# Attention with hashed buckets and two MLPs on one core: loads, bits, placing, conversions and the last copies in another order

## The chip, the cores and the metric

One core of a Trainium2 chip runs the whole program in one launch. Its engines are TensorE (PE, with its weight loads as PEld), VectorE (DVE), ScalarE (ACT), GpSimd (POOL) and SyncE (SP, which here only issues DMA transfers, in the order of the program). Each engine works through its own list of instructions in order and waits on semaphores for the others. The metric is the device time of one execution, in microseconds (us).

## The reference

Three stages: attention and two MLPs. The weights of the MLPs are float64 and reach the kernel as 64-bit words; all other inputs are float32.

```python
def _attn_ref(q, k, v, proj):                 # q, k, v: (2, 8, 768, 64), proj: (64, 6)
    scale = 1.0 / np.sqrt(D)
    q_bits = (np.einsum('bhsd,dk->bhsk', q, proj) > 0).astype(np.int64)
    k_bits = (np.einsum('bhsd,dk->bhsk', k, proj) > 0).astype(np.int64)
    powers = 2 ** np.arange(n_bits)
    q_bucket = np.sum(q_bits * powers, axis=-1)
    k_bucket = np.sum(k_bits * powers, axis=-1)
    mask = q_bucket[:, :, :, None] == k_bucket[:, :, None, :]
    scores = scale * np.matmul(q, k.transpose(0, 1, 3, 2))
    scores = np.where(mask, scores, -1000000000.0)
    scores = scores - np.max(scores, axis=-1, keepdims=True)
    attn = np.exp(scores)
    attn = attn / (np.sum(attn, axis=-1, keepdims=True) + 1e-09)
    return np.matmul(attn, v).astype(np.float32)

def reference(...):
    attn_out = _attn_ref(**attn_kwargs)
    x = np.ascontiguousarray(attn_out.transpose(0, 2, 1, 3)).reshape(B * S, H * D)   # 1536 x 512
    h = np.maximum(x @ w_in, 0.0);  x = h * h @ w_out          # 512 -> 2048 -> 512
    h = x @ w2_in;  return (h * np.tanh(softplus(h))) @ w2_out # 512 -> 2048 -> 512
```

## The kernel before

**Pairs and steps.** The 16 heads (2 batches of 8) go in 8 pairs `p`. A pair has 12 steps (`PER`), each a tile of 128 query rows of one head against all 768 keys; there are 96 steps (`N`), in groups of three (`QT`) that share one accumulator. The loop at the end of the listing runs over the steps `j`. Every large number is kept as a rounded part and a remainder (`qh`/`ql`, `kh`/`kl`, `ph`/`pl`), and products are summed over both. One step does, in this order of the code:

- the DMA issues and GpSimd work that a table `calls` has for this step (`at(j, f)` adds to it);
- PE: `scores(j + 2)`, four matmuls from `QA`, `KA` and `QB`, `KB` (L365, L367); the last 12 rows of `QB` and `KB` hold the hash bits, so that a bucket that differs makes the score a huge number;
- ACT: `exponent(j + 1)` (L382);
- if bits are under way: their negation on ACT (L291);
- if a group of three is finished: `unstack` copies its sums out of PSUM on ACT, for the first head of a pair into `hi` (L434), for the second into `both` (L439). Only one `both` buffer exists; in the next step `place` moves its halves by DMA into `hi` and `lo` (L442, L443), and `finish` later adds and scales on GpSimd into `xf`, the input of the MLPs;
- DVE: `lower(j - 1)`, the remainder `pl` (L409), which frees the PSUM buffer of the transposes `pT`;
- if bits are under way: `compare` on DVE (L294) and one GpSimd operation (L295);
- PE: `transpose(j)`, six transposes `pT` (L392), and where a half of a pair is done the six sums as a row (L394);
- DVE: `clamp(j + 2)` (L373), which frees the PSUM buffer of the scores;
- ACT: `upper(j)`, the rounded part `ph` (L405);
- PE: `pv` of the group before (L421), four matmuls into `acc`;
- in one step of each pair: `bits_split` (L286), eight matmuls that give the next pair's hash bits, from `qh`, `ql`, `kh`, `kl`;
- the `next(conv)` calls that a list `conv_at` has for this step.

Scores, transposes and bits share three PSUM buffers (`ps2`), taken in turn.

**The next pair.** While pair `p` is worked on, pair `p + 1` is made ready by a `plan` of steps: `load` of `q_r`, `k_r` and `v_r` (L156, L161), `split_q` and `split_k` on GpSimd (L311, L312, L328 to L330: `qh`, `ql`, `kh`, `kl`) and `split_v` (L345, L346), `place_q`, `place_k` (DMA into `QA`, `KA`, `QB`, `KB`; L321, L339) and `place_bits` (L304, L305). Pair 0 has a plan of its own, since its own inputs are loaded only at the start.

**Weights.** The MLP weights arrive as 64-bit words and are turned into float32 by hand, in pieces of 128 x 512, by the generator `weights()`: a load `stg` (L83), Abs (L117 on ACT), a clamp and a shift (L121, L122 on DVE), two or-operations (L124, L126 on DVE), and two GpSimd operations that split the result (L127, L128). Each `next(conv)` advances it by one `yield`, a quarter of a piece. Five pieces are done beside the attention, the others within the MLPs.

**The end.** After the loop come the row of the last reciprocals (`rT` on PE, `rs` on ACT, L453), the last `pl`, and with `early.close()` the buffers of attention are released; `split` makes `xs` from the finished block of `xf` (L615, L616), the last sums are accumulated, and the MLPs begin with the matmuls `h` (L642 to L644).

Of the kernel before, what the change touches and what calls it, by code (L numbers as in the profile page):

```python
# [17 lines left out]
P = 128  # L18
# [9 lines left out]

LAG = 5

WARM = 3

F64_LOW = 3.4332275390625e-05
F64_HIGH = 122879.9921875
# [3 lines left out]
def lsh_attention_relu2_mish_kernel(ctx, tc, qT, kT, vP, proj, w_in, w_out, w2_in, w2_out, out):  # L38
# [16 lines left out]
    def b32(ap):  # L55
        return ap.bitcast(F32)
# [29 lines left out]
    def weights():  # L86

        pieces = [
            (i, nm, src, c)
            for i in range(2 * G)  # L90
            for nm, src in (("i", (w_in, w2_in)[i // G]), ("o", (w_out, w2_out)[i // G]))
            for c in range(FC)
        ]
        staged = {}

        def stage(k):
            if k not in staged and k < len(pieces):
                i, _, src, c = pieces[k]
                staged[k] = fetch(src, c, i % G)

        stage(0)
        yield
        for k, (i, nm, _, c) in enumerate(pieces):
            if c == 0:
                W[i, nm] = wpools[i % 2].tile([P, 2, FC, 512], F32R, tag="w" + nm, name=f"w{nm}{i}")
            t = W[i, nm]
            s = staged.pop(k)
            for n in range(k + 1, k + 1 + len(stage_pools)):
                stage(n)

            words = s.bitcast(U32).rearrange("p (n t) -> p n t", t=2)
            lo, hi = words[:, :, 0], words[:, :, 1]
            hf = s.bitcast(F32).rearrange("p (n t) -> p n t", t=2)[:, :, 1]
            m = stg.tile([P, 512], F32, tag="cv", name="cv")
            mu = m.bitcast(U32)
            if loaded[-1] == EXP_SET:
                nc.scalar.activation(m, hf, AF.Abs)  # L117
            else:
                nc.vector.scalar_tensor_tensor(m, hf, -1.0, hf, ALU.mult, ALU.max)
            yield  # L120
            nc.vector.tensor_scalar(m, m, F64_LOW, F64_HIGH, ALU.max, ALU.min)  # L121
            nc.vector.tensor_scalar(mu, mu, 3, 0x3FFFFFF8, ALU.logical_shift_left, ALU.bitwise_and)  # L122
            yield
            nc.vector.scalar_tensor_tensor(mu, lo, 29, mu, ALU.logical_shift_right, ALU.bitwise_or)  # L124
            yield
            nc.vector.scalar_tensor_tensor(mu, hi, 0xC0000000, mu, ALU.bitwise_and, ALU.bitwise_or)  # L126
            nc.gpsimd.tensor_scalar(t[:, 0, c, :], m, 1.0, 0.0, ALU.mult, ALU.add)  # L127
            nc.gpsimd.tensor_tensor(t[:, 1, c, :], m, b32(t[:, 0, c, :]), ALU.subtract)  # L128
            yield
# [16 lines left out]
    one = early.enter_context(tc.tile_pool(name="one", bufs=1))  # L146
    qk = early.enter_context(tc.tile_pool(name="qk", bufs=3))
    pm = early.enter_context(tc.tile_pool(name="pm", bufs=3))
    ps2 = early.enter_context(tc.tile_pool(name="ps2", bufs=3, space=PSUM))

    sgs, rawt, heads, vst, v_rs = {}, {}, {}, {}, {}

    def load(p, nm):

        t = raw.tile([P, S], F32, tag=nm, name=nm)
        nc.sync.dma_start(out=t, in_=(qT if nm == "q_r" else kT)[p])  # L156
        rawt[p] = rawt.get(p, ()) + (t,)
# [201 lines left out]
    def scores(j):  # L359
        p, half, hh, t = seq[j]  # L360
        QA, QBt, KA, KBt = heads[p, hh]
        q0 = half * H2 + t * P
        ps = sc[j] = ps2.tile([P, 1024], F32, tag="ps2", name="s")
        for c0, c1 in ((0, 512), (512, S)):
            nc.tensor.matmul(ps[:, c0:c1], QA[:, q0:q0 + P], KA[:, c0:c1], start=True, stop=False)  # L365
        for c0, c1 in ((0, 512), (512, S)):
            nc.tensor.matmul(ps[:, c0:c1], QBt[:, q0:q0 + P], KBt[:, c0:c1], start=False, stop=True)  # L367

# [43 lines left out]
    def pv(g, n):  # L412

        p, half, hh, _ = seq[g * QT]
        if n == 0:
            accs[g] = ps1.tile([P, H2], F32, tag="ps1", name="acc")
        per = 2 * KT // QT
        for k in range(n * per, (n + 1) * per):
            c = k % KT
            w = vst[p][:, hh * KT + c, :]  # L420
            nc.tensor.matmul(accs[g], w, phl[g][k // KT][:, c, :], start=k == 0, stop=k == 2 * KT - 1)  # L421
# [3 lines left out]
    def unstack(g, j):  # L425

        p, half, hh, _ = seq[g * QT]
        acc = accs.pop(g)
        del phl[g]
        if hh == 0:  # L430
            hi = xt.tile([P, H2], F32, tag="hi", name="hi")
            lo = xt.tile([P, H2], F32, tag="lo", name="lo")
            hl[p, half] = hi, lo
            nc.scalar.activation(hi, acc, AF.Copy)  # L434
            at(j + 1, lambda: nc.sync.dma_start(out=lo[0:D], in_=hi[D:P]))
        else:
            hi, lo = hl[p, half]
            both = xt.tile([P, H2], F32, tag="both", name="both", bufs=1)
            nc.scalar.activation(both, acc, AF.Copy)  # L439

            def place():
                nc.sync.dma_start(out=hi[D:P], in_=both[0:D])  # L442
                nc.sync.dma_start(out=lo[D:P], in_=both[D:P])  # L443

            at(j + 1, place)
            at(j + 4 + 2 * (j == N), lambda: finish(p, half))

    rbs = {}
# [28 lines left out]

    calls = {}

    def at(j, f):  # L480
        calls.setdefault(j, []).append(f)

    bits_at = {}
    for p in range(NP - 1):
        o, n = p * PER, p + 1
        if p == 0:
            plan = ((3, split_q, (n,)), (4, split_k, (n,)), (5, place_q, (n, 0)), (6, place_k, (n, 0)),
                    (6, place_q, (n, 1)), (7, place_k, (n, 1)), (8, place_bits, (n, 0)), (8, place_bits, (n, 1)),
                    (8, split_v, (n,)), (8, load, (n + 1, "q_r")), (8, load, (n + 1, "k_r")), (11, load_v, (n + 1,)))
            bits_at[o + 6] = n  # L490
        else:
            plan = ((1, place_k, (n, 0)), (2, load, (n + 1, "q_r")), (3, load, (n + 1, "k_r")), (3, split_v, (n,)),
                    (7, place_bits, (n, 0)), (7, place_q, (n, 1)), (8, place_bits, (n, 1)), (8, place_k, (n, 1)),
                    (10, load_v, (n + 1,)))
            bits_at[o + 4] = n
        plan += (9, split_q, (n + 1,)), (10, split_k, (n + 1,)), (11, place_q, (n + 1, 0))
        for m, f, args in plan:
            if args[0] < NP:
                at(o + m, lambda f=f, args=args: f(*args))

    conv_at = [5, 6, 6, 8, 10] + [b for b in bits_at if b > PER for _ in range(2)] + [N - PER + m for m in (1, 4, 6, 8)]

    kb = head_bits(0, 1, 0, S)
    head_k(0)
# [40 lines left out]
    split_v(0)  # L545
    load(1, "q_r")
    load(1, "k_r")
    load_v(1)
    split_proj()
    waiting, bits, sums = None, None, None  # L550
    for j in range(N):
        for f in calls.pop(j, ()):
            f()
        if j + 2 < N:
            scores(j + 2)
        if j + 1 < N:
            exponent(j + 1)
            sums = next((k for k, last in ends.items() if last == j + 1), None)
            if sums is not None:
                add_tiny(sums)  # L560
        if bits is not None:
            bits[0]()
        if waiting is not None:
            unstack(waiting, j)
            waiting = None
        if j:
            lower(j - 1)
        if bits is not None:
            bits[1]()
            bits = None  # L570
        if j == 1:
            head_qbits(1, 0, S, qb1)
        done = next(iter(r6s), None)
        transpose(j, r6s.get(done))
        if j + 2 < N:
            clamp(j + 2)
        if sums is not None:
            nc.vector.reciprocal(tiny[sums], tiny[sums])
            if j + 2 < N:
                r6s[sums] = tiny[sums]  # L580
            sums = None
        upper(j)
        if done is not None:
            del r6s[done]
            broadcast(*done, pts[j][:2 * QT, S:S + P], j)
        g, n = divmod(j, QT)
        if g:
            pv(g - 1, n)
            if n == QT - 1:
                waiting = g - 1  # L590
        if j == 0:
            qb1 = head_bits(1, 0, 0, S)
        if j in bits_at:
            bits = bits_split(bits_at[j])
        for _ in range(conv_at.count(j)):
            next(conv)
    for f in calls.pop(N, ()):
        f()
    ps = ps2.tile([P, 1024], F32, tag="ps2", name="rT")
    done = seq[N - 1][:2]  # L600
    r6 = tiny[done]
    nc.tensor.transpose(ps[:2 * QT, 0:P], r6, ident)
    lower(N - 1)
    broadcast(*done, ps[:2 * QT, 0:P], N)
    unstack(waiting, N)
    early.close()

    act = ctx.enter_context(tc.tile_pool(name="act", bufs=NBLK, reuse_waits="tile"))
# [7 lines left out]
            nc.vector.tensor_tensor(t[:, 1, c, :], src[:, c, :], b32(t[:, 0, c, :]), ALU.subtract)  # L616

    xs = {}
    split((0, 0), xf[0])
    for n in range(QT):  # L620
        pv(N // QT - 1, n)
    unstack(N // QT - 1, N)
    for j in sorted(calls):
        for f in calls[j]:
# [163 lines left out]
```

## Time and profile before

| | us |
|---|---|
| median of 3 runs | 762.97 (762.72 to 763.2) |
| the profiled execution | 762.05 |
| its span | 759.9 |
| PE busy | 745.8 |
| DVE busy | 534.5 |
| ACT busy | 358.0 |
| POOL busy | 263.9 |

Busy times are sums over the span of one profiled execution; 762.05 is the time of that execution itself, of which the span is the part between its first and last instruction. The mean TensorE clock granted was 0.997 of full speed.

### The profile page before, as it was taken

The page shows a single profiled execution, that of the slowest core. Times are in us where ns is not written, and L with a number is a line of the kernel's source. Part 1 is how long each engine was busy: PE and PEld are TensorE (multiplying, and loading weights), DVE is VectorE, ACT ScalarE, POOL GpSimd, SP SyncE. Part 2 cuts the span into 40 slices and gives each one's busy share as a digit, 9 for nine tenths or more (in the row PEclk, how much of TensorE's full clock was granted, in tenths as well). Part 3 has the DMA queues.
Part 4 walks back from the last instruction along what each step waited for, and adds up shares of the span by engine and source line. Part 5 has one row for each costly group of instructions (what it writes and reads, how often), then busy time and mean ns, then how long its engine had stood idle before and what let it go on. Part 6 is the DMA issues. An engine that isn't in the chain of part 4 may idle for free.

```text
span 759.9 us, 10509 instructions
## 1 busy us (share of the span) xinstructions
PE 745.8 (98%) x3742; PEld 635.5 (84%) x3742; DVE 534.5 (70%) x859; ACT 358.0 (47%) x640; POOL 263.9 (35%) x261
## 2 busy tenths in 40 slices
PE   8889999999999999999999999999999999999997
PEld 4779999999998888888888888888888888888886
DVE  8878988988997966566566688978454767566223
ACT  6878889889897443423233213333223121212120
POOL 9464555655223433232232232224223222232100
PEclk9999999999999999999999999999999999999999
DMA  5775696678423122122121122112212111120013
GB/s 145 196 207 157 167 232 158 167 203 193 108 71 92 56 84 82 57 69 70 56 84 55 56 68 67 60 56 84 84 55 81 59 56 56 56 83 28 1 55 111
DMA packets 28956, 72.69 MB, mean 96 GB/s; under 512 B 5048, under 2 KB 10264, under 8 KB 28904
## 3 DMA queue, kind: packets, MB, share of 16 engines
q1 hardware_dynamic: 28824, 72.01, 33.5%
q8 instruction: 30, 0.49, 0.3%
q14 instruction: 22, 0.18, 0.1%
q10 hardware_dynamic: 80, 0.00, 0.0%
HBM read 46.14 MB, written 3.19 MB: 65 GB/s over the span
## 4 chain that ended last, share of the span: by engine, by line
PE 86%; DMA 4%; DVE 3%; ACT 2%; POOL 2%; issue 2%; SPq 0%; DVEq 0%; ACTq 0%; POOLq 0%
PE h L642 11%; PE h L644 11%; PE h L643 11%; PE pT L392 6%; PE acc L421 6%; PE acc L688 6%; PE acc L689 6%; PE acc L690 6%; PE acc L696 6%; PE acc L695 6%; PE acc L694 6%; PE s L367 3%; PE s L365 3%; DVE pl L409 1%; ACT ph L405 1%
## 5 line engine op out<-in xcount | busy, mean ns | idle before, releaser
L643 PE MATMUL h<-xs,wi 128*128 128x512 f32 x384 | 149.4, 389 | 0.0
L644 PE MATMUL h<-xs,wi 128*128 128x512 f32 x384 | 149.4, 389 | 0.0
L642 PE MATMUL h<-xs,wi 128*128 128x512 f32 x384 | 149.4, 389 | 0.0
L668 ACT ACTIVATE g<-h 128x512 f32<-128x512 f32 x48 | 28.7, 598 | 188.7 <-PE h L644 172.0
L409 DVE TENSOR_TENSOR pl<-pT,ph 128x768 fp32r<-128x768 f32 x96 | 91.7, 956 | 20.1 <-ACT ph L405 13.4
L652 ACT ACTIVATE r<-h 128x512 f32<-128x512 f32 x48 | 28.7, 598 | 153.3 <-PE h L644 153.3
L127 POOL TENSOR_SCALAR wo<-cv 128x512 fp32r<-128x512 f32 x32 | 29.4, 918 | 194.3 <-DVE cv L126 178.9
L382 ACT ACTIVATE e<-e,nm 128x768 f32<-128x768 f32 x96 | 89.8, 936 | 6.0 <-DVE e L373 5.5
L673 DVE TENSOR_TENSOR gl<-g,gh 128x512 fp32r<-128x512 f32 x48 | 35.9, 748 | 80.6 <-ACT gh L670 80.6
L373 DVE TENSOR_SCALAR_CACHE_REDUCE e<-s 128x768 f32<-128x768 f32 x96 | 91.0, 947 | 0.9 <-PE s L367 0.8
L654 DVE TENSOR_TENSOR s<-r 128x512 f32<-128x512 f32 x48 | 38.8, 808 | 70.2 <-ACT r L652 70.2
L405 ACT ACTIVATE ph<-pT 128x768 fp32r<-128x768 f32 x96 | 77.7, 809 | 18.2 <-PE pT L394 10.1
L644 PEld LDWEIGHTS h<-xs,wi 128*128 128x128 f32 x384 | 72.1, 188 | 15.1
L642 PEld LDWEIGHTS h<-xs,wi 128*128 128x128 f32 x384 | 72.1, 188 | 14.9
L643 PEld LDWEIGHTS h<-xs,wi 128*128 128x128 f32 x384 | 72.0, 188 | 14.8
L392 PE MATMUL pT<-ident,e 128*128 128x128 f32 x576 | 79.1, 273 | 3.6 <-DVE pl L409 3.2
L127 POOL TENSOR_SCALAR wi<-cv 128x512 fp32r<-128x512 f32 x32 | 27.3, 854 | 147.5 <-DVE cv L126 147.5
L392 PEld LDWEIGHTS pT<-ident,e 128*128 128x128 f32 x576 | 66.3, 140 | 11.2 <-ACT r L386 1.9
L688 PE MATMUL acc<-gh,wo 128*128 128x512 f32 x192 | 74.7, 389 | 0.0
L689 PE MATMUL acc<-gl,wo 128*128 128x512 f32 x192 | 74.7, 389 | 0.0
L690 PE MATMUL acc<-gh,wo 128*128 128x512 f32 x192 | 74.7, 389 | 0.0
L694 PE MATMUL acc<-wo,gh 128*128 128x512 f32 x192 | 74.7, 389 | 0.0
(111 smaller groups left out, 1413.8 us busy)
## 6 DMA issues: line engine op xcount, KB each, us to landing
stg<-in_w_in_dram SPq DMA_DIRECT2D x32, 512.0 KB
stg<-in_w_out_dram SPq DMA_DIRECT2D x32, 512.0 KB
KA<-kh SPq DMA_DIRECT2D x28, 192.0 KB
v_r<-in_vP_dram SPq DMA_DIRECT2D x8, 384.0 KB
rb<-rd SPq DMA_DIRECT2D x32, 96.0 KB
out_dram<-tot SPq DMA_DIRECT2D x12, 256.0 KB
q_r<-in_qT_dram SPq DMA_DIRECT2D x7, 384.0 KB
k_r<-in_kT_dram SPq DMA_DIRECT2D x7, 384.0 KB
```

What stands on the lines that cost most here:

```text
L373: nc.vector.tensor_scalar(e, ps[:, 0:S], MASKED, None, ALU.min, ALU.min, accum_out=nm)
L382: nc.scalar.activation(e, e, AF.Exp, bias=nm, scale=-1.0, accum_out=ssums[p, half][:, c:c + 1])
L392: nc.tensor.transpose(ps[:, c * P:(c + 1) * P], e[:, c * P:(c + 1) * P], ident)
L405: nc.scalar.activation(ph, v, AF.Copy)
L409: nc.vector.tensor_tensor(pl, v, b32(ph), ALU.subtract)
L642: nc.tensor.matmul(h, w[:, 0, fi, cs], xs[:, 0, c, :], start=c == 0, stop=False)
L643: nc.tensor.matmul(h, w[:, 0, fi, cs], xs[:, 1, c, :], start=False, stop=False)
L644: nc.tensor.matmul(h, w[:, 1, fi, cs], xs[:, 0, c, :], start=False, stop=c == PPB - 1)
L688: nc.tensor.matmul(y, w[:, 0, fi, cs], gh, start=fi == 0, stop=False)
L689: nc.tensor.matmul(y, w[:, 0, fi, cs], gl, start=False, stop=False)
L690: nc.tensor.matmul(y, w[:, 1, fi, cs], gh, start=False, stop=fi == FC - 1)
L694: nc.tensor.matmul(o, gh[:, qs], w[:, 0, fi, :], start=fi == 0, stop=False)
```

## The change

- Pair 0's plan: the loads of `q_r` and `k_r` of pair 2 move from step 8 to step 4, that of `v_r` from 11 to 9; the first `place_k` of pair 1 goes from step 6 to 5, its second from 7 to 8, the bits' placing from step 8 to 7. Pair 1's bits are computed in step 5, not 6. In pair 1's plan the loads of pair 3 go from steps 2 and 3 to 4 and 5.
- The placing of `both` is put first among its step's calls.
- `next(conv)` is called between `lower(j - 1)` and the bits' comparison, not at the step's end; the first load of a weight piece goes ahead of `load_v(1)`; the steps in `conv_at` are others.
- Four of the five early weight pieces have Abs and clamp as three GpSimd operations.
- `scores(0)` has two matmuls of zeros between its two halves.
- At the end: `clamp(95)` stands ahead of `lower(92)`; the sums' copies `unstack(29)`, `unstack(30)`, the row `rs` and `unstack(31)` come among and behind the `xs` copies; the last reciprocals are made on DVE alone; the last accumulator sits in a `ps2` buffer.

```diff
+EARLY = 5
+FILL = 2
@@ weights
-            if loaded[-1] == EXP_SET:
+            if 0 < k < EARLY:
+                nc.gpsimd.tensor_scalar(m, hf, 0.0, -2.0, ALU.min, ALU.mult)
+                nc.gpsimd.tensor_tensor(m, m, hf, ALU.add)
+                nc.gpsimd.tensor_scalar(m, m, F64_LOW, F64_HIGH, ALU.max, ALU.min)
+            elif loaded[-1] == EXP_SET:
                 nc.scalar.activation(m, hf, AF.Abs)
...
-            nc.vector.tensor_scalar(m, m, F64_LOW, F64_HIGH, ALU.max, ALU.min)
+            if not 0 < k < EARLY:
+                nc.vector.tensor_scalar(m, m, F64_LOW, F64_HIGH, ALU.max, ALU.min)
@@ pools
-    ps2 = early.enter_context(tc.tile_pool(name="ps2", bufs=3, space=PSUM))
+    ps2 = late.enter_context(tc.tile_pool(name="ps2", bufs=3, space=PSUM))
@@ scores
+        for _ in range(FILL * (j == 0)):
+            nc.tensor.matmul(ps[:, 0:H2], zero[:, 0:P], zero, start=False, stop=False)
@@ unstack
-            both = xt.tile([P, H2], F32, tag="both", name="both", bufs=1)
+            if g < N // QT - 1:
+                both = xt.tile([P, H2], F32, tag="both", name="both", bufs=1)
+            else:
+                both = b32(pt.tile([P, KT, H2], F32R, tag="ph", name="both")[:, 0, :])
...
-            at(j + 1, place)
+            at(j + 1, place, j < N)
@@ calls
-    def at(j, f):
-        calls.setdefault(j, []).append(f)
+    def at(j, f, first=False):
+        c = calls.setdefault(j, [])
+        c.insert(0 if first else len(c), f)
...
         if p == 0:
-            plan = ((3, split_q, (n,)), (4, split_k, (n,)), (5, place_q, (n, 0)), (6, place_k, (n, 0)),
-                    (6, place_q, (n, 1)), (7, place_k, (n, 1)), (8, place_bits, (n, 0)), (8, place_bits, (n, 1)),
-                    (8, split_v, (n,)), (8, load, (n + 1, "q_r")), (8, load, (n + 1, "k_r")), (11, load_v, (n + 1,)))
-            bits_at[o + 6] = n
+            plan = ((3, split_q, (n,)), (4, split_k, (n,)), (4, load, (n + 1, "q_r")), (4, load, (n + 1, "k_r")),
+                    (5, place_q, (n, 0)), (5, place_k, (n, 0)), (6, place_q, (n, 1)), (7, place_bits, (n, 0)),
+                    (7, place_bits, (n, 1)), (8, place_k, (n, 1)), (8, split_v, (n,)), (9, load_v, (n + 1,)))
+            bits_at[o + 5] = n
         else:
-            plan = ((1, place_k, (n, 0)), (2, load, (n + 1, "q_r")), (3, load, (n + 1, "k_r")), (3, split_v, (n,)),
+            m = 2 if p > 1 else 4
+            plan = ((1, place_k, (n, 0)), (m, load, (n + 1, "q_r")), (m + 1, load, (n + 1, "k_r")), (3, split_v, (n,)),
...
-    conv_at = [5, 6, 6, 8, 10] + [b for b in bits_at if b > PER for _ in range(2)] + [N - PER + m for m in (1, 4, 6, 8)]
+    conv_at = [4, 6, 6]
+    for p in range(1, NP - 1):
+        conv_at += [p * PER + m for m in ((4, 6) if p % 2 else (4, 5))]
+    conv_at += [N - PER - 4, N - PER - 3] + [N - PER + m for m in (2, 3, 6)]
@@ the loop
+    next(conv)
     load_v(1)
...
-        if waiting is not None:
+        if waiting is not None and j < N - QT:
             unstack(waiting, j)
             waiting = None
+        if j == N - 3:
+            clamp(j + 2)
+        if j == N - 1:
+            done = seq[j][:2]
+            r6 = sm.tile([P, 2 * QT], F32, tag="r6", name="r6", bufs=2)
+            nc.vector.tensor_scalar(r6, ssums.pop(done), 1e-9, None, ALU.add)
+            nc.vector.reciprocal(r6, r6)
         if j:
             lower(j - 1)
+        for _ in range(conv_at.count(j)):
+            next(conv)
         if bits is not None:
             bits[1]()
...
-        for _ in range(conv_at.count(j)):
-            next(conv)
@@ the end
+    rp = ps2.tile([P, 1024], F32, tag="ps2", name="rT")[:2 * QT, 0:P]
+    nc.tensor.transpose(rp, r6, ident)
     lower(N - 1)
-    broadcast(*done, ps[:2 * QT, 0:P], N)
-    unstack(waiting, N)
+    accs[N // QT - 1] = ps2.tile([P, 1024], F32, tag="ps2", name="acc")[:, 0:H2]
+    for n in range(QT):
+        pv(N // QT - 1, n)
     early.close()
...
-    split((0, 0), xf[0])
-    for n in range(QT):
-        pv(N // QT - 1, n)
+    split((0, 0), xf[0], 0, 2)
+    unstack(waiting, N - 1)
+    for f in calls.pop(N):
+        f()
+    split((0, 0), xf[0], 2)
+    unstack(N // QT - 2, N)
+    broadcast(*done, rp, N)
     unstack(N // QT - 1, N)
```

What the edits move is seen in the order of the instructions on an engine (the lines of the changed kernel are its own, so L409 there is L420, and so on). First, SP's transfers around pair 2's loads (`q_r`, `k_r`) and pair 1's placing. Before:

```order
L156 DMA k_r<-in_kT_dram 128x768
L161 DMA v_r<-in_vP_dram 128x768
L321 DMA QA<-qh 64x768
L321 DMA QA<-ql 64x768
L321 DMA QB_126<-qh 64x768
L83 DMA stg<-in_w_in_dram 128x512
L339 DMA KA<-kh 64x768 x2
L339 DMA KB_130<-kl 64x768
L321 DMA QA<-qh 64x768
```

Of the change:

```order
L165 DMA k_r<-in_kT_dram 128x768
L87 DMA stg<-in_w_in_dram 128x512
L170 DMA v_r<-in_vP_dram 128x768
L165 DMA q_r<-in_qT_dram 128x768
L165 DMA k_r<-in_kT_dram 128x768
L87 DMA stg<-in_w_in_dram 128x512
L330 DMA QA<-qh 64x768
L330 DMA QA<-ql 64x768
L330 DMA QB_126<-qh 64x768
L348 DMA KA<-kh 64x768 x2
L348 DMA KB_130<-kl 64x768
```

Two loads of pair 2 and a second weight piece now stand ahead of the first placing; before, the loads came behind the placing of pair 1's bits. Further on, SP's transfers when the `both` of pair 0 is placed, in the first steps of pair 1. Before:

```order
L455 DMA rd<-rs 6x128
L339 DMA KA<-kh 64x768 x2
L339 DMA KB_128<-kl 64x768
L442 DMA hi<-both 64x384
L443 DMA lo<-both 64x384
L156 DMA q_r<-in_qT_dram 128x768
L156 DMA k_r<-in_kT_dram 128x768
L442 DMA hi<-both 64x384
```

Of the change:

```order
L469 DMA rd<-rs 6x128
L456 DMA hi<-both 64x384
L457 DMA lo<-both 64x384
L348 DMA KA<-kh 64x768 x2
L348 DMA KB_128<-kl 64x768
L456 DMA hi<-both 64x384
L457 DMA lo<-both 64x384
L165 DMA q_r<-in_qT_dram 128x768
```

The first two transfers of `both` go ahead of `KA` and `KB` of pair 2, and the second two ahead of the loads of pair 3. On DVE, the steps around pair 1's bits (`q_r<-bits` is the comparison, `cv` the weight piece). Before:

```order
L409 TENSOR_TENSOR pl<-pT,ph 128x6x128
L373 TENSOR_SCALAR e,nm<-s 128x768
L121 TENSOR_SCALAR cv<-cv 128x512
L122 TENSOR_SCALAR cv<-cv 128x512
L409 TENSOR_TENSOR pl<-pT,ph 128x6x128
L294 TENSOR_TENSOR q_r<-bits,k_r 48x768
L373 TENSOR_SCALAR e,nm<-s 128x768
L578 RECIPROCAL r_455<-r_455 128x6
L409 TENSOR_TENSOR pl<-pT,ph 128x6x128
L373 TENSOR_SCALAR e,nm<-s 128x768
L124 SCALAR_TENSOR_TENSOR cv<-stg,cv 128x512
```

Of the change:

```order
L384 TENSOR_SCALAR e,nm<-s 128x768
L420 TENSOR_TENSOR pl<-pT,ph 128x6x128
L130 TENSOR_SCALAR cv<-cv 128x512
L131 TENSOR_SCALAR cv<-cv 128x512
L133 SCALAR_TENSOR_TENSOR cv<-stg,cv 128x512
L303 TENSOR_TENSOR q_r<-bits,k_r 48x768
L384 TENSOR_SCALAR e,nm<-s 128x768
L420 TENSOR_TENSOR pl<-pT,ph 128x6x128
L384 TENSOR_SCALAR e,nm<-s 128x768
L607 RECIPROCAL r_465<-r_465 128x6
```

The conversion stands behind the `pl` and ahead of the comparison, with the or-operation that came three clamps later. Last, ACT at the end of attention. Before:

```order
L405 ACTIVATE ph<-pT 128x6x128 x2
L453 ACTIVATE rs<-rT 6x128
L434 ACTIVATE hi<-acc 128x384
L615 ACTIVATE xs<-xf_74 128x512 x4
L439 ACTIVATE both<-acc 128x384
L117 ACTIVATE cv<-stg 128x512
```

Of the change:

```order
L416 ACTIVATE ph<-pT 128x6x128 x2
L639 ACTIVATE xs<-xf_74 128x512 x2
L453 ACTIVATE both<-acc 128x384
L639 ACTIVATE xs<-xf_74 128x512 x2
L445 ACTIVATE hi<-acc 128x384
L467 ACTIVATE rs<-rT 6x128
L453 ACTIVATE both<-acc 128x384
L125 ACTIVATE cv<-stg 128x512
```

The `xs` copies come first, and `rs`, which was ahead of them, stands behind two copies of sums.

## Rows read from the trace of the kernel before

**Rows 1.** The page: busy us, share of the span, instructions of each engine

```profile
PE 745.8 (98%) x3742; PEld 635.5 (84%) x3742; DVE 534.5 (70%) x859; ACT 358.0 (47%) x640; POOL 263.9 (35%) x261
```

**Rows 2.** Windows: us, busy PE PEld DVE ACT POOL, clock, DMA share, GB/s

```profile
12.00:22.00 10.00, 9.48 (x54) 6.86 (x53) 9.77 (x16) 7.68 (x15) 9.42 (x15) 1.00 0.58 168
...
22.00:36.00 14.00, 12.40 (x85) 11.46 (x84) 11.45 (x20) 11.45 (x21) 5.84 (x5) 1.00 0.94 240
...
50.00:60.00 10.00, 6.79 (x34) 5.84 (x33) 5.07 (x11) 5.29 (x10) 3.81 (x3) 0.83 0.69 200
...
300.00:350.00 50.00, 50.00 (x223) 41.40 (x222) 29.29 (x48) 17.55 (x30) 15.72 (x14) 1.00 0.23 74
...
56.39:59.81 3.42, 3.42 (x14) 2.96 (x13) 2.69 (x7) 2.35 (x5) 0.00 (x0) 0.50 0.65 213
```

**Rows 3.** Timeline around pair 1's bits: start, duration, instruction, [idle before <-releaser]

```profile
22.58 1.85 POOL L330 TENSOR_TENSOR kl<-k_r,kh 128x768 fp32r<-128x768 f32 x1
...
28.66 0.67 ACT L117 ACTIVATE cv<-stg 128x512 f32<-128x512 f32 x1 [0.94 <-DMA stg<-in_w_in_dram]
...
29.37 0.43 DVE L121 TENSOR_SCALAR cv<-cv 128x512 f32<-128x512 f32 x1 [1.83 <-ACT cv L117]
...
31.27 0.84 PE L392 MATMUL pT<-ident,e 128*128 128x128 f32 x6 [1.60 <-DVE pl L409]
...
31.36 0.95 DVE L294 TENSOR_TENSOR q_r<-bits,k_r 48x768 f32<-48x768 f32 x1 [0.23 <-ACT k_r L291]
...
34.92 1.76 DVE L124 SCALAR_TENSOR_TENSOR cv<-stg,cv 128x512 uint32<-128x512 uint32 x1
...
38.57 0.84 PE L392 MATMUL pT<-ident,e 128*128 128x128 f32 x6
```

**Rows 4.** Timeline around pair 2's loads and bits

```profile
36.66 0.51 SPq L156 DMA_DIRECT2D q_r<-in_qT_dram  x1
...
40.40 1.12 POOL L311 TENSOR_SCALAR qh<-q_r 128x768 fp32r<-128x768 f32 x1 [4.27 <-DMA q_r<-in_qT_dram]
...
48.95 0.82 SPq L443 DMA_DIRECT2D lo<-both  x1
...
51.02 0.82 PE L392 MATMUL pT<-ident,e 128*128 128x128 f32 x6
...
53.42 0.49 ACT L439 ACTIVATE both<-acc 128x384 f32<-128x384 f32 x1 [3.90 <-DMA lo<-both]
...
55.75 0.58 PE L286 MATMUL bits<-qh,pwr 128*112 128x512 f32 x2 [3.21 <-POOL xf L474]
...
61.65 0.82 PE L392 MATMUL pT<-ident,e 128*128 128x128 f32 x6
```

**Rows 5.** Timeline around a later pair's bits

```profile
82.29 0.82 PE L392 MATMUL pT<-ident,e 128*128 128x128 f32 x6
...
83.78 0.65 DVE L124 SCALAR_TENSOR_TENSOR cv<-stg,cv 128x512 uint32<-128x512 uint32 x1
...
86.08 0.87 PE L392 MATMUL pT<-ident,e 128*128 128x128 f32 x6 [0.19 <-DVE pl L409]
...
88.30 0.81 PE L392 MATMUL pT<-ident,e 128*128 128x128 f32 x6
```

**Rows 6.** Timeline from the last exponent to the first matmul of the MLPs

```profile
228.64 0.94 ACT L382 ACTIVATE e<-e,nm 128x768 f32<-128x768 f32 x1 [0.24 <-DVE e L373]
...
231.44 0.27 ACT L453 ACTIVATE rs<-rT 6x128 f32<-6x128 f32 x1
...
231.98 2.18 ACT L615 ACTIVATE xs<-xf 128x512 fp32r<-128x512 f32 x4
...
233.70 0.39 PE L642 MATMUL h<-xs,wi 128*128 128x512 f32 x1
```

**Rows 7.** Timeline of the start

```profile
1.32 4.11 PE L208 MATMUL zeros<-zero 128*128 128x384 f32 x6 [1.32 <-DVE zero L184]
...
9.54 0.58 PE L367 MATMUL s<-KB,QB 128*128 128x512 f32 x2 [1.20 <-DVE QB L262]
```

More of the change, by code (lines that the diff above doesn't have):

```diff
@@ L414, in pv @@
         p, half, hh, _ = seq[g * QT]
-        if n == 0:
+        if n == 0 and g not in accs:
             accs[g] = ps1.tile([P, H2], F32, tag="ps1", name="acc")
@@ L557, in lsh_attention_relu2_mish_kernel @@
             exponent(j + 1)
-            sums = next((k for k, last in ends.items() if last == j + 1), None)
+            sums = next((k for k, last in ends.items() if last == j + 1 < N - 1), None)
             if sums is not None:
@@ L572, in lsh_attention_relu2_mish_kernel @@
             head_qbits(1, 0, S, qb1)
-        done = next(iter(r6s), None)
-        transpose(j, r6s.get(done))
-        if j + 2 < N:
+        ready = next(iter(r6s), None)
+        transpose(j, r6s.get(ready))
+        if j + 3 < N:
             clamp(j + 2)
@@ L578, in lsh_attention_relu2_mish_kernel @@
             nc.vector.reciprocal(tiny[sums], tiny[sums])
-            if j + 2 < N:
-                r6s[sums] = tiny[sums]
+            r6s[sums] = tiny[sums]
             sums = None
         upper(j)
-        if done is not None:
-            del r6s[done]
-            broadcast(*done, pts[j][:2 * QT, S:S + P], j)
+        if ready is not None:
+            del r6s[ready]
+            broadcast(*ready, pts[j][:2 * QT, S:S + P], j)
         g, n = divmod(j, QT)
@@ L588, in lsh_attention_relu2_mish_kernel @@
             pv(g - 1, n)
-            if n == QT - 1:
+            if n == QT - 1 and j < N - 1:
                 waiting = g - 1
@@ L594, in lsh_attention_relu2_mish_kernel @@
             bits = bits_split(bits_at[j])
-        for _ in range(conv_at.count(j)):
-            next(conv)
[L597 to L602, printed above, removed]
+    rp = ps2.tile([P, 1024], F32, tag="ps2", name="rT")[:2 * QT, 0:P]
+    nc.tensor.transpose(rp, r6, ident)
     lower(N - 1)
-    broadcast(*done, ps[:2 * QT, 0:P], N)
-    unstack(waiting, N)
+    accs[N // QT - 1] = ps2.tile([P, 1024], F32, tag="ps2", name="acc")[:, 0:H2]
+    for n in range(QT):
+        pv(N // QT - 1, n)
     early.close()
```

## Prediction

> **What bounds the kernel now.** I read the page's summary first: TensorE (PE) is busy 745.8 us, 98% of the span [rows 1], so only some 14 us can come from PE's idle time, and the question is where that lies. The windows say where: once the MLP part runs, PE is busy 50.00 of 50.00 us, but 12.40 of 14.00 us at 22 to 36 and 6.79 of 10.00 us at 50 to 60, where the mean granted clock is 0.83 [rows 2]. In the MLP there is nothing to gain: its end follows its first `h` matmul at a fixed distance, so the forecast is the shift of that matmul. The timeline then shows what PE waits for in three kinds of places, each tied to the `bits` of the next pair of heads.
>
> The first place is pair 1's bits [rows 3]. At 28.66 ACT has stood 0.94 us for a weight piece still on its way, DVE then 1.83 us for ACT's Abs (29.37), and only after the two conversion operations that follow does DVE do the `pl` that frees a PSUM buffer, so the transposes of step 7 start at 31.27, after 1.60 us of idle PE. At 34.92 an or-operation takes 1.76 us. Step 10's transposes come at 38.57.
>
> The second place is pair 2's [rows 4]. Its `q_r` is issued at 36.66; GpSimd stands 4.27 us for it and starts to split at 40.40. The two transfers that empty the only `both` buffer stand in SP's queue behind `KA` and `KB` of that pair, which wait for the split; the second goes out at 48.95. ACT waits 3.90 us for it (53.42), and so does all that follows on ACT. PE idles 3.21 us before the bits at 55.75, and from 56.39 to 59.81 runs at the lower of its two clock levels, 0.50 of full [rows 2]. The transposes of step 16 are at 51.02, those of step 18 at 61.65: 10.63 us.
>
> The third kind are the five later pairs' bits. The same two steps take 6.01 us there, from 82.29 to 88.30 [rows 5]. Weight conversion stands in DVE's queue ahead of `pl` (an or-operation of 0.65 at 83.78, against the 1.76 of 34.92, and a second like it), and PE idles 0.19 us for `pl` at 86.08.
>
> **The change part by part.** Six undisturbed steps, 38.57 to 51.02, take 12.45 us: 2.075 each [rows 3, 4].
>
> *First place.* The bits come one step earlier. They need `kl`, which ends at 24.43 (22.58 + 1.85 [rows 3]), so they can follow step 5's work on PE. The piece's Abs stands in step 4 now, on a load put far ahead, so its 0.94 and most of 1.83 us of waiting go; its 0.67 us reaches DVE at most once, and I put the `pl` of step 5, which in this order is the one ahead of the conversion, to end at 27.0. Behind it come two operations of 0.43 (as at 29.37) and an or of 0.69 at most: 28.55. Then the comparison, 0.95 (as at 31.36): 29.5. Then the clamp of step 8, taken as equally long: 30.45, which releases the buffer for step 7's transposes: 30.45 against 31.27. Three undisturbed steps more give 36.7 for step 10, against 38.57, as no or-operation stands behind: **−1.85**. Bounds: −0.75, if the or-operation in the bits' way takes 1.76; −2.5, if the Abs is wholly hidden.
>
> *Second place.* `q_r` and `k_r` of pair 2 are issued in the place of step 4, near 17, and not at 36.66. GpSimd's 4.27 us go, and with the 1.85 gained before, the split ends some 6 us sooner. The `both` transfers now stand ahead of `KA`, so nothing holds them once ACT has written the buffer. ACT asks for it again at 53.42 − 3.90 − 1.85 = 47.7; they have several us for 96 KB each, and ACT's wait and PE's 3.21 us go. With no such idle time no row gives a reason for the half clock: PE's 1.60 us without work [rows 3] stand in a window at 1.00 [rows 2]. Step 16 then comes at 51.02 − 1.85 = 49.2 and step 18 some 6.05 later, 55.25, against 61.65: 6.4, so **−4.55** beyond the first term. Bounds: −5.2, if this bits place is free of an or-operation as well (0.65 less); −2.5, if half of the stall stays.
>
> *Later bits, five of them.* For three pairs two or-operations (0.65 each) move from before `pl` to behind it, so PE's transposes don't wait for them; but they still stand ahead of the comparison and the clamp, whose buffers the next steps need. Of 1.3 us I take 0.30 back for each. The other two lose an Abs on ACT (0.67) and a 0.43 us operation on DVE, with the same chain left: 0.24 each. Sum **−1.4**; bounds −0.95 (five times PE's 0.19) and −2.4.
>
> *Conversion on GpSimd.* Four pieces take three GpSimd operations in place of Abs and clamp. The trace has none of these; between 0.85 us each (below half of the 1.85 at 22.58, with one input of two) and 1.85. GpSimd is busy 3.81 of 10.00 us at 50 to 60 [rows 2] and takes 2.5 to 5 us a piece beside other work: 0. With that cover gone, the operation that follows each comparison on GpSimd would be late by as much, and what waits for it, the placing of the bits, has more than a step (2.075) of slack.
>
> The Trainium skill ("SBUF — State Buffer", section "Who interferes with whom") says that a DVE instruction with two SBUF inputs and a GpSimd instruction that reads SBUF shut one another out for a whole instruction. The or of 1.76 us at 34.92, which reads two SBUF tiles, agrees. By that rule alone, with one or lengthened as there, the sum below would be −6.0; by the row at 83.78 [rows 5] it is −7.1.
>
> *Zeros in the first scores.* Two matmuls of 384 columns. Six records of their like took 4.11 us at the half clock [rows 7], that is 0.34 each at the full one; two matmuls are four records, 1.37 us, in the 1.20 us that PE waits for `QB` ahead of 9.54: **0**, bounds 0 and +0.17.
>
> *The end.* The clamp of step 95 goes ahead of a `pl`, so the exponent, which waited for it (228.64 [rows 6]), and all up to the last sums come about 0.5 us sooner; some **−0.1** falls away in the steps before. But the row of reciprocals, `rs`, that ACT copied at 231.44, ahead of all, is now copied behind four `xs` pieces, a `both` and a `hi`; the `rT` it reads sits in PSUM that the first `h` takes over, so `h` waits for it. ACT: end of the last `ph`, where `rs` began before, 231.44 − 0.5 = 230.94; `xs` 2.18; `both` 0.49 [rows 4], `hi` as much; `rs` 0.27: 234.4. Then `h`, near 234.5, against 233.70 [rows 6]: **+0.8**. Bounds: −0.5, if it waits for `xs` alone, and +1.2.
>
> Sum: −1.85 − 4.55 − 1.4 − 0.1 + 0.8 = −7.1 us. The profiled execution took 762.05 us, 2.15 of it around its span; that gives 754.95. The median of the runs shown, 762.97, is 0.92 longer, so I predict **755.9 us**.
>
> **The rivals.** A: pair 1's transfers come late. `q_r` and `k_r` (384 KB each) and a weight piece (512 KB) now go ahead of pair 1's placing. At the 240 GB/s of 22 to 36, where the DMA engines are 0.94 busy [rows 2], 1.29 MB are 5.4 us. For it: that window is nearly full. Against: from 12 to 22 the engines were 0.58 busy at 168 GB/s [rows 2], which leaves room for most. If 2 us of it reach the first scores of pair 1: 757.9. Chance 0.2.
>
> B, the other side, one step further: the early loads take 168 GB/s, 7.7 us, and none of it is absorbed. Scores due at 36 wait that long and, after more than 3.21 us of idle PE, run at the half clock: 3.42 us of work at half rate, +1.7. That makes 755.9 + 9.4 = 765.3. It decides from a delay of 7.1 us on. Chance 0.03.
>
> C: ors meet GpSimd's added operations, as at 34.92: +1.1 at one place, 757.0. For it that row; against it that GpSimd's part of a piece comes ahead of DVE's. Chance 0.12.
>
> D: `h` doesn't wait for `rs`, or later bits give back their full 2.4: 754.6 to 754.9, both 753.6. For it: before, `h` started with no copy just ended. Chance 0.17.
>
> E: half of the second stall stays, 758, or nothing is gained there, 760.5: other transfers ahead of `both`'s could hold it as before. Chance 0.08.
>
> **How the numbers follow.** The forecast has 0.40, with a spread of its own of 755.1 to 756.7. The range reaches down to 753.4 for D and up to 759.0 for A, C and half of E, and leaves out 0.1 to 0.2. Less than about 0.2% (1.5 us) can't be told from no change. Faster by more than that 0.94: all but B and the ends of A and E; the same 0.03; slower 0.03.
>
> **What would show it.** After the change: the transposes of step 7 near 30.5, of step 10 near 36.7; pair 2's `q_r` issued near 17; no wait of `both` for a transfer, no PE clock below full between 40 and 60, and step 18 near 55.3; first `h` near 226.6 (233.70 − 7.1), with `rs` as what released it. I am wrong if scores at 35 to 37 wait for a DMA (A, B), if an or-operation of over 1 us stands in the bits' way (C), or if `h` starts right behind the last `acc` (D).

## The result, and the profile after

The changed kernel takes 755.77 us (median of five runs, 755.43 to 757.0; a sixth, disturbed, took 933.41 at a mean clock of 0.753 and is left out) against 762.85 us before (762.32 to 764.67). The ratio is 0.9907, with a 95% interval of 0.9893 to 0.992: faster by 6.1 to 8.2 us, where 7.1 were forecast. The sum was right; what follows shows that two of its terms were not.

The page after, by engine (compare [rows 1]), and the group of the first `h` matmuls with its idle time:

```profile
PE 747.6 (99%) x3746; PEld 634.6 (84%) x3746; DVE 532.9 (71%) x856; ACT 356.6 (47%) x635; POOL 285.6 (38%) x273
...
L670 PE MATMUL h<-xs,wi 128*128 128x512 f32 x384 | 149.5, 389 | 0.6 <-ACT rs L467 0.6
```

Windows of the changed kernel (compare [rows 2]; columns as there, busy us of PE, PEld, DVE, ACT, POOL, then clock, DMA share, GB/s):

```profile
22.00:36.00 14.00, 13.85 (x92) 12.56 (x91) 12.90 (x24) 12.47 (x24) 7.76 (x8) 1.00 0.70 173
50.00:60.00 10.00, 9.74 (x64) 8.34 (x63) 8.53 (x14) 7.92 (x17) 8.72 (x8) 1.00 0.62 190
300.00:350.00 50.00, 50.00 (x223) 41.40 (x222) 27.38 (x47) 17.55 (x31) 13.65 (x12) 1.00 0.20 64
```

PE's idle time in the two early stretches is down from 1.60 to 0.15 and from 3.21 to 0.26 us, no clock is below full there, and the DMA engines of 22 to 36 are less busy than before (0.70 against 0.94). GpSimd works 8.72 of 10 us instead of 3.81. No scores at 30 to 50 waited for a transfer, so rivals A and B didn't come.

The timeline after, first place (compare [rows 3]):

```profile
24.25 0.66 ACT L125 ACTIVATE cv<-stg 128x512 f32<-128x512 f32 x1
...
25.64 0.96 DVE L420 TENSOR_TENSOR pl<-pT,ph 128x768 fp32r<-128x768 f32 x1 [0.56 <-ACT ph L416]
...
27.38 0.95 DVE L420 TENSOR_TENSOR pl<-pT,ph 128x768 fp32r<-128x768 f32 x1
28.25 0.42 DVE L130 TENSOR_SCALAR cv<-cv 128x512 f32<-128x512 f32 x1
...
29.17 0.69 DVE L133 SCALAR_TENSOR_TENSOR cv<-stg,cv 128x512 uint32<-128x512 uint32 x1
...
29.78 0.94 DVE L303 TENSOR_TENSOR q_r<-bits,k_r 48x768 f32<-48x768 f32 x1
...
31.65 0.87 PE L403 MATMUL pT<-ident,e 128*128 128x128 f32 x6
...
37.97 0.82 PE L403 MATMUL pT<-ident,e 128*128 128x128 f32 x6
```

The Abs costs DVE 0.56 us once, ahead of step 4's `pl` (25.64). Behind step 5's `pl` (27.38) the weights' clamp (28.25), shift, or and the comparison follow without a gap, as the prediction's chain has it. Second place (compare [rows 4]):

```profile
17.25 0.38 SPq L165 DMA_DIRECT2D q_r<-in_qT_dram  x1
...
44.42 0.48 SPq L456 DMA_DIRECT2D hi<-both  x1
...
48.80 0.47 ACT L453 ACTIVATE both<-acc 128x384 f32<-128x384 f32 x1
...
50.40 0.82 PE L403 MATMUL pT<-ident,e 128*128 128x128 f32 x6
...
50.63 1.02 POOL L483 TENSOR_TENSOR hi<-hi,lo 128x384 f32<-128x384 f32 x1
50.92 1.27 DVE L135 SCALAR_TENSOR_TENSOR cv<-stg,cv 128x512 uint32<-128x512 uint32 x1
...
56.88 0.87 PE L403 MATMUL pT<-ident,e 128*128 128x128 f32 x6
```

`q_r` is issued at 17.25, the transfers of `both` are out by 44.42, and ACT's copy at 48.80 waits for nothing. The or-operation at 50.92 is stretched to 1.27 beside a GpSimd sum. And the end (compare [rows 6]):

```profile
228.15 0.49 ACT L445 ACTIVATE hi<-acc 128x384 f32<-128x384 f32 x1
228.52 0.25 ACT L467 ACTIVATE rs<-rT 6x128 f32<-6x128 f32 x1
...
228.82 0.50 PE L670 MATMUL h<-xs,wi 128*128 128x512 f32 x1 [0.58 <-ACT rs L467]
```

All absolute times of this profile are 1.65 us late: its first transposes are at 14.58, those of before at 12.93. So the stages are compared by differences between rows of `pT` (steps are counted from 0) and the first `h`, in us; from that `h` to the end of the span it is 526.23 us before and 526.36 after:

| | first `pT` | to step 10 | 10 to 18 | 18 to 78 | 78 to 93 | 93 to `h` | first `pT` to `h` |
|---|---|---|---|---|---|---|---|
| before | 12.93 | 25.64 | 23.08 | 133.93 | 31.13 | 6.99 | 220.77 |
| changed | 14.58 | 23.39 | 18.91 | 132.49 | 32.04 | 7.41 | 214.24 |
| difference | +1.65 | −2.25 | −4.17 | −1.44 | +0.91 | +0.42 | −6.53 |

### The profile page after: what moved, and what is told of

The parts are those of the page before. It is cut to its first block, busy times and chain, and to the rows that moved or that the text cites. A ratio compares the mean times of both kernels' runs of the same rounds, so it can differ in the third digit from the quotient of the medians.

```text
span 755.2 us, 10541 instructions
## 1 busy us (share of the span) xinstructions
PE 747.6 (99%) x3746; PEld 634.6 (84%) x3746; DVE 532.9 (71%) x856; ACT 356.6 (47%) x635; POOL 285.6 (38%) x273
## 4 chain that ended last, share of the span: by engine, by line
PE 95%; DVE 3%; ACT 1%; issue 1%; ACTq 0%
PE h L670 12%; PE h L671 12%; PE h L672 12%; PE acc L432 8%; PE pT L403 8%; PE acc L717 6%; PE acc L718 6%; PE acc L716 6%; PE acc L722 6%; PE acc L724 6%; PE acc L723 6%; PE s L378 4%; PE s L374 4%; PE bits L295 1%; DVE e L384 1%
## 5 line engine op out<-in xcount | busy, mean ns | idle before, releaser
L420 DVE TENSOR_TENSOR pl<-pT,ph 128x768 fp32r<-128x768 f32 x96 | 91.4, 953 | 15.9 <-ACT ph L416 10.0
L393 ACT ACTIVATE e<-e,nm 128x768 f32<-128x768 f32 x96 | 89.9, 936 | 15.0 <-DVE e L384 14.7
L722 PE MATMUL acc<-wo,gh 128*128 128x512 f32 x192 | 74.7, 389 | 0.0
L723 PE MATMUL acc<-wo,gh 128*128 128x512 f32 x192 | 74.7, 389 | 0.0
```

Source lines behind the costliest of these rows:

```text
L393: nc.scalar.activation(e, e, AF.Exp, bias=nm, scale=-1.0, accum_out=ssums[p, half][:, c:c + 1])
L420: nc.vector.tensor_tensor(pl, v, b32(ph), ALU.subtract)
L722: nc.tensor.matmul(o, gh[:, qs], w[:, 0, fi, :], start=fi == 0, stop=False)
L723: nc.tensor.matmul(o, gh[:, qs], w[:, 1, fi, :], start=False, stop=False)
```

## The experiments

All times are medians; kernels named together ran on one chip with the kernel before.

**The changed kernel again, without zeros, with rs early, and a better version** (before 762.62).

> The changed kernel once more. In its profile PE's clock rose at 7.32 us, before it at 5.19, and the first transposes were 1.65 us late (14.58 against 12.93), before any of the changed instructions. Theory: that moment varies between executions, so it may come at 5.19 here, the profiled execution then takes 755.4 us, and counted from the first transposes every step stands as before (step 18 at 42.30, first h at 214.24). Rival: something in the change sets it; then the clock rises at 7.32 again and the profiled execution takes 757.

Measured 755.74 (ratio 0.9905, 0.989 to 0.992), the profiled execution 755.49. The clock rose at 4.21 this time, first `pT` at 12.96, from there 23.39 to step 10, 42.28 to step 18 and 214.37 to `h`. So the change doesn't fix the late start; whether it makes it more frequent is open. Over the 14 profiles of this study the clock rises between 4.1 and 7.4 us (4.6 to 6.3 in those built on the kernel before) and the first `pT` comes at 12.7 to 14.7.

```diff
-FILL = 2
+FILL = 0
```

> The changed kernel without the two matmuls of zeros in the first scores. Theory: they lie in time in which PE waits for QB anyway, so nothing changes (755.9, within 0.5), and PE idles about 1.2 us there again. Rival: the zeros are what makes the start 1.65 us late; then 754.3 and the first transposes at 12.9.

Measured 756.25 (755.23 to 756.85; ratio 0.9911, 0.9894 to 0.9928). What its profile shows was in neither theory. PE's scores and two windows, of this kernel:

```profile
9.93 0.59 PE L378 MATMUL s<-KB,QB 128*128 128x512 f32 x2 [1.90 <-DVE QB L271]
...
9.00:11.00 2.00, 1.07 (x6) 0.97 (x7) 1.20 (x3) 0.48 (x1) 1.92 (x3) 0.99 0.04 1
11.00:14.40 3.40, 3.40 (x9) 1.83 (x8) 2.52 (x6) 2.06 (x4) 3.24 (x3) 0.50 0.73 157
```

After 1.90 us of idle PE the clock fell back to half, from 10.98 to 14.39, and the first `pT` came at 14.69 although the clock had first risen at 4.15. The changed kernel with zeros, with its clock up as early (4.21), kept it and had its first `pT` at 12.96.

```diff
+    broadcast(*done, rp, N)
     split((0, 0), xf[0], 2)
     unstack(N // QT - 2, N)
-    broadcast(*done, rp, N)
```

> The changed kernel with the copy of the last reciprocals' row (rs) ahead of the second half of the xs copies. Theory: the first h waits 0.58 us for rs alone, so it comes 0.5 to 0.6 sooner, 755.3, and starts with no wait over 0.1. Rival: with rs out of the way it waits as long for another copy of ACT or for PSUM, and nothing changes (755.9).

Measured 755.03 (754.28 to 756.05; ratio 0.9897, 0.988 to 0.9914), 0.7 below the changed kernel beside it; the intervals overlap, but the trace shows the gain:

```profile
225.96 0.25 ACT L467 ACTIVATE rs<-rT 6x128 f32<-6x128 f32 x1
226.12 1.14 ACT L639 ACTIVATE xs<-xf 128x512 fp32r<-128x512 f32 x2
226.92 0.39 PE L670 MATMUL h<-xs,wi 128*128 128x512 f32 x1
```

`h` starts with no wait shown, 6.65 us after step 93 instead of 7.41: the copy of `rs` was the wait, and it cost 0.76.

```diff
-        for _ in range(conv_at.count(j)):
+        for _ in range(conv_at.count(j) * (j < N - 17)):
             next(conv)
         if bits is not None:
             bits[1]()
...
             bits = bits_split(bits_at[j])
+        for _ in range(conv_at.count(j) * (j >= N - 17)):
+            next(conv)
```

> The changed kernel with rs early and the conversion calls of the last 16 steps at the end of their step again, as in the kernel before. Theory: the five calls there lengthen the last pair's steps by 0.88 us over 2.05 each, the calls at the step's end by about 0.25; so 0.6 less there and 0.55 less at the end: 754.7. Rival: the lengthening goes with the DVE work itself wherever it stands, as DVE has no time left in a step; then 755.3, from rs alone.

Measured 754.62 (753.87 to 755.2; ratio 0.9887, 0.9868 to 0.9906). The medians of this version and the one before it differ by 0.4, within their intervals; the profiles tell them apart. Steps 78 to 93 take 31.11 us here and 31.90 to 32.20 in the seven profiles with the same five calls ahead of the transposes (31.92 with `rs` early alone). So the rival falls: the calls cost 0.8 to 1.1 us ahead of the transposes. Behind them they cost nothing that shows: the five steps that have one take 2.05 or 2.06 us here, as undisturbed steps do. In the changed kernel, at such a step, and in this version, at the same step:

```profile
208.32 0.85 PE L403 MATMUL pT<-ident,e 128*128 128x128 f32 x6
...
208.97 0.68 DVE L133 SCALAR_TENSOR_TENSOR cv<-stg,cv 128x512 uint32<-128x512 uint32 x1
...
209.56 0.95 DVE L384 TENSOR_SCALAR_CACHE_REDUCE e<-s 128x768 f32<-128x768 f32 x1
...
210.66 0.85 PE L403 MATMUL pT<-ident,e 128*128 128x128 f32 x6
```

```profile
208.08 0.82 PE L403 MATMUL pT<-ident,e 128*128 128x128 f32 x6
...
209.50 0.69 DVE L133 SCALAR_TENSOR_TENSOR cv<-stg,cv 128x512 uint32<-128x512 uint32 x1
210.13 0.82 PE L403 MATMUL pT<-ident,e 128*128 128x128 f32 x6
```

In the first the or-operation pushes the clamp (209.56), and the transposes come 2.34 us after the last ones (208.32); in the second they stay 2.05 apart.

**The second place, by one edit at a time** (before 762.98).

```diff
-            at(j + 1, place)
+            at(j + 1, place, True)
```

> The kernel before with one edit: the two transfers that empty both go first among their step's calls, ahead of KA and KB of the next pair. Theory 1 (what stalls ACT at 53.42 is the order of SP's queue alone): the 3.90 us wait, PE's 3.21 us and the half clock go, step 18 comes 4.5 us sooner counted from the first transposes (44.2 instead of 48.72), the time is about 758.3. Theory 2 (the late loads carry it: q_r at 36.66 makes all of pair 2 late): the split's end near 47.1 still holds the bits; no more than 1.5 us are won, 761.3.

Here `place` is first in every step, the last one too, where it goes ahead of the copy `lo<-hi` that reads what it overwrites: the last half pair's sums are therefore others. Measured 759.07 (ratio 0.9951, 0.9937 to 0.9966). Steps 10 to 18 take 19.16 us instead of 23.08, step 18 is at 44.53 from the first `pT`. Both as theory 1 had them, though 0.8 slower than its 758.3; steps 78 to 93 take 31.97 in its profile (below).

```diff
-... (4, split_k, (n,)), ... (8, load, (n + 1, "q_r")), (8, load, (n + 1, "k_r")), ...
+... (4, split_k, (n,)), (4, load, (n + 1, "q_r")), (4, load, (n + 1, "k_r")), ...
```

> The kernel before with one edit: q_r and k_r of pair 2 are loaded in pair 0's step 4, not 8. Theory 1: GpSimd's 4.27 us wait shrinks, the split ends 3 to 4 us sooner, so KA goes out near 43 and both behind it near 45, before ACT asks for the buffer at 49.5: this edit alone removes the stall as well, step 18 at 44.2 from the first transposes, 758.3. Theory 2: the loads delay pair 1's placing by their 768 KB instead, and PE waits some 2 us at the scores of steps 12 to 14: 760 or more.

Measured 757.97 (ratio 0.9945, 0.9928 to 0.9962). Steps 10 to 18 take 18.78: theory 1 again. The way to step 10 is 0.29 longer (25.93), in step 9, which takes 3.31 instead of 3.05 us; the version with `place` first, without early loads, has 3.28 there, so this can't be put down to the loads.

```diff
-            at(j + 1, place, j < N)
+            at(j + 1, place)
```

> The changed kernel with both's transfers behind KA and KB of the next pair again. Theory 1 (early loads suffice too): the split ends near 42, KA and KB go out some 2 us before both, both near 47 at the latest, ACT waits under 0.5 us, step 18 at 42.3 to 42.8 from the first transposes. Theory 2 (the order carries it): ACT waits 2 us or more for both and PE idles.

```diff
-... (4, split_k, (n,)), (4, load, (n + 1, "q_r")), (4, load, (n + 1, "k_r")), ...
+... (4, split_k, (n,)), ... (8, split_v, (n,)), (8, load, (n + 1, "q_r")), (8, load, (n + 1, "k_r")), ...
```

> The changed kernel with the loads of q_r and k_r of pair 2 in pair 0's step 8 again. Theory 1 (the order of both suffices): counted from the first transposes step 18 stays at 42.3 within 0.4. Theory 2 (the loads carry it): it comes 2 us later or more, with PE idle before bits.

One profiled run each. Steps 10 to 18 take 19.95 and 20.27 instead of 18.91: with one of the two edits taken back, 1.0 and 1.4 us return. ACT's copies into `both`, with `place` last and with late loads:

```profile
50.50 0.49 ACT L453 ACTIVATE both<-acc 128x384 f32<-128x384 f32 x1 [1.51 <-DMA lo<-both]
```

```profile
48.83 0.49 ACT L453 ACTIVATE both<-acc 128x384 f32<-128x384 f32 x1 [1.57 <-DMA lo<-both]
```

Theory 1's size falls here (0.4 to 0.5 at most), theory 2's too. In the kernel before either edit alone removes the stall; in the changed kernel, where ACT asks for the buffer some 2.4 us sooner after the first `pT` (34.2 instead of 36.6), it takes both.

**Conversions and zeros** (before 762.83).

```diff
-EARLY = 5
+EARLY = 0
```

> The changed kernel with Abs on ACT and the clamp on DVE for all pieces, as before the change. Theory: GpSimd's operations cost nothing and took 0.43 us of DVE work out of two even pairs' bits and Abs out of odd pairs' steps; without them 0.3 to 0.9 us more in all, 756.5. Rival (the shared port: GpSimd's additional operations lengthen DVE's): without them the time falls, 755.4 or less.

Measured 759.16 (758.6 to 760.44; ratio 0.9953, 0.9937 to 0.997), 3.4 us above the changed kernel's 755.77. Neither theory: the rival is refuted, and the price is several times the one I gave. Steps 18 to 78 take 135.06 us instead of 132.49, 78 to 93 32.90 instead of 32.04. An Abs on ACT, two steps after bits, and what it does:

```profile
57.14 0.65 ACT L125 ACTIVATE cv<-stg 128x512 f32<-128x512 f32 x1
...
58.52 0.96 DVE L420 TENSOR_TENSOR pl<-pT,ph 128x768 fp32r<-128x768 f32 x1 [0.98 <-ACT ph L416]
...
60.49 0.85 PE L403 MATMUL pT<-ident,e 128*128 128x128 f32 x6
```

`pl` waits 0.98 us for ACT, and the transposes at 60.49 come 2.53 after the last ones (57.96), not 2.05. Three odd pairs lose this (0.5 each), and three even ones 0.35 by DVE's clamp ahead of the bits: 2.6. In the changed kernel GpSimd spends 2.00, 1.32 and 1.93 us on the three operations instead.

```diff
+        for _ in range(FILL * (j == 0)):
+            nc.tensor.matmul(ps[:, 0:H2], zero[:, 0:P], zero, start=False, stop=False)
```

> The kernel before with the two zero matmuls in its first scores. Theory: the kernel before is in the same danger (1.20 us of idle PE at 8.3 to 9.5) but its own profile shows no fall; so the median stays within 0.5 of 762.8, and its longest runs (764.6) go. Rival: the zeros win a half clock's price in most executions: 761.3.

Measured 761.92 (761.08 to 764.96; ratio 0.9989, 0.9978 to 0.9999, so only just clear of none). The theory's size falls by a little (0.9, not 0.5), the rival's 1.5 is not reached, and the longest run did not go. Its profile doesn't tell why: its first `pT` is at 13.45, and it gained in the second place (21.79 for steps 10 to 18), where PE idled 2.42 and not 3.21 us and the clock stayed up. It lost 0.85 in steps 78 to 93, at one operation:

```profile
217.09 1.01 POOL L473 TENSOR_TENSOR hi<-hi,lo 128x384 f32<-128x384 f32 x1 [7.72 <-DMA lo<-both]
217.11 1.27 DVE L124 TENSOR_SCALAR cv<-cv 128x512 uint32<-128x512 uint32 x1
```

In the kernel with `place` first the same shift stood beside the same sum and took 1.26, which is its 0.8 as well.

```diff
-    conv_at += [p * PER + m for m in ((4, 6) if p % 2 else (4, 5))]
+    conv_at += [p * PER + m for m in ((6, 6) if p == 1 else (4, 6) if p % 2 else (4, 5))]
```

> The version with rs early and the last pair's conversion at the step's end, and with the or-operation of step 16 moved to step 18, behind pair 2's bits and away from GpSimd's sum of hi and lo beside which it took 1.27 us. Theory (it is this operation that makes steps 16 to 18 longer, 6.47 where later odd pairs take 5.89): step 18 comes 0.5 to 0.6 sooner counted from the first transposes (41.7), 754.1. Rival: the bits' negation on ACT is what the comparison waits for, and with or without that operation step 18 stays at 42.3.

Measured 753.9 (753.58 to 755.22; ratio 0.9886, 0.9871 to 0.99): the same as the version without this edit, within the intervals. Steps 10 to 18 take 18.16 instead of 18.89, as the theory has it, but steps 18 to 78 take 133.37 instead of 132.49, since pair 2's bits now meet the same thing with another operation:

```profile
75.25 1.84 POOL L355 TENSOR_TENSOR vs<-v_r,vs 128x768 fp32r<-128x768 f32 x1
...
76.31 1.06 DVE L131 TENSOR_SCALAR cv<-cv 128x512 uint32<-128x512 uint32 x1
```

From the first `pT` to `h` it is 212.66 us here, 212.51 without the edit. The wait was moved, not removed.

> The changed kernel without zeros in the first scores, once more. In the first such run PE was idle 1.90 us ahead of the first QB scores, the clock fell to half at 10.98 to 14.39, and the first transposes came at 14.69. Theory 1: without the zeros this idle time lowers the clock whenever the start is early; again half clock, first transposes near 14.7. Theory 2: it happens in some executions only; then near 13.0 and no fall.

First `pT` at 14.63, but because the clock rose only at 7.34; it did not fall after that, though PE idled nearly as long:

```profile
11.25 0.58 PE L378 MATMUL s<-KB,QB 128*128 128x512 f32 x2 [1.84 <-DVE QB L271]
```

Theory 1 asked for an early start and this was none, so the run decides nothing between them.

## Why the prediction was right, and where it wasn't

*First place*, −1.85 forecast, −2.25 measured. The rows agree with the chain link by link; the term was somewhat small, mostly because step 5's `pl` ended 0.3 us earlier after the first `pT` than I put it (28.33 − 14.58 = 13.75 instead of 27.0 − 12.93 = 14.07). No run takes this place's edits one by one, so what each of them is worth is not shown.

*Second place*, −4.55 forecast, −4.17 measured. The mechanism was right: `both`'s transfers were late, and without them ACT, PE and the clock have no stall. The missing 0.4 is the or-operation of 1.27 at 50.92 (without it, in the last version above, steps 16 to 18 take 5.73 instead of 6.47). That is the sign which the prediction named for rival C, an or-operation of over 1 us in the bits' way, at about half of C's price; but it met the sum of `hi` and `lo`, which is not one of the operations that the change adds. The Trainium skill's "SBUF — State Buffer", section "Who interferes with whom", says that a DVE instruction with two SBUF inputs contends with a GpSimd instruction that reads SBUF. The traces agree: 1.27 beside GpSimd's sum, 0.68 for the like at 208.97.

*Later bits* with *conversion on GpSimd*, −1.4 and 0 forecast, −1.44 measured for both. The number was right and its assignment was wrong. I booked 0.9 on the or-operations' new place and only 0.48 on Abs and clamp leaving ACT and DVE. With Abs and clamp left on ACT and DVE, the new order is 1.13 us slower in steps 18 to 78 than before (135.06 against 133.93); GpSimd's operations give 2.57 back. That rests on one profile without them and eight with them (132.48 to 132.50), and on the 3.4 us between the medians.

*The end*, −0.1 and +0.8 forecast, +0.91 and +0.42 measured. The failing step is "some −0.1 falls away in the steps before": I counted the operations that the last 16 steps lose and not that the five calls there now stand ahead of the clamp, where they cost 0.8 to 1.1 us in all. The version with the calls put back shows it (31.11 for steps 78 to 93). Before `h` the mechanism was right and the term too large: 0.42. The wait for `rs` costs 0.76; against that, step 95's transposes come 1.36 us behind step 94's and not 1.65. The earlier clamp would do that, but no run tests it alone.

*Zeros*, 0 forecast. The medians are 0.5 (without them, in the changed kernel; within the intervals) and 0.9 us (with them, in the kernel before; at the interval's edge) in their favour. One profile shows a mechanism, a fall to half clock after 1.90 us of idle PE at the start. How often it happens stays open.

These terms make −6.53 (−6.40 by the repeated run); the medians differ by 7.08. Of the rest, 0.35 lies outside the span: the profiled execution of before took 2.15 us more than its span, that of the changed kernel 757.0 − 755.2 = 1.8. What it is no run here shows; the kernel before with early loads alone has 1.8 as well (1.79 to 1.87 in four runs), with `place` first alone 2.1. So the total was met by errors that cancel: the first place gave 0.4 more than forecast and the time outside the span another 0.35; the second place gave 0.4 less, and the end cost 0.6 more.

## What to carry to other kernels

In a kernel with a full pipeline, the place of an operation in its step is worth more than its length: the same five calls cost 0.8 to 1.1 us ahead of the transposes and nothing that shows behind them. Where a buffer of one waits for transfers behind a slow producer in one DMA queue, either sending them first or making the producer earlier may do; test them one by one, since a gain elsewhere can make both necessary. And when a sum comes out right, take its terms apart all the same.

## What was not expected of the hardware

The shift at 217.11 in the kernel with zeros has one SBUF input, and took 1.27 us beside a GpSimd sum that had begun 0.02 us earlier; the same shift in the kernel before took 0.43 where both began at 218.21, and there the GpSimd sum was stretched to 1.30 and steps 78 to 93 were 0.85 shorter:

```profile
218.21 1.30 POOL L469 TENSOR_TENSOR hi<-hi,lo 128x384 f32<-128x384 f32 x1 [7.52 <-DMA lo<-both]
218.21 0.43 DVE L122 TENSOR_SCALAR cv<-cv 128x512 uint32<-128x512 uint32 x1
```

I had counted only operations with two SBUF inputs as exposed. The same section of the Trainium skill's "SBUF — State Buffer" counts `tensor_scalar` among the operations that can take the shared ports as well, and says that whoever issues first holds them for its whole instruction. The pair at 217.09 and 217.11 agrees, GpSimd being first and DVE lengthened. In the pair at 218.21 GpSimd is lengthened, but the rows don't show that DVE was first. Two other points: GpSimd took 2.00 us for its first new operation and 1.93 for its third, above the upper end of 1.85 that I had set; and the clock first rises anywhere from 4.1 to 7.4 us in these profiles, and two executions of the changed kernel itself, with the rise at 4.21 and 7.32, have their first transposes at 12.96 and 14.58: 1.62 us apart, more than several of the terms.
